# The attention's weighted sums in four visits per unit instead of eight, and one transpose a slot later

## The chip, the cores and the metric

The kernel runs on one core of one Trainium2 chip. The metric is device microseconds (us) of one execution. A profiled execution also has a span, from its first to its last instruction. The engines are TensorE (PE in the rows; PEld are its weight loads), VectorE (DVE), ScalarE (ACT), GpSimd (POOL) and SyncE (SP), which here issues every DMA.

## What is computed

Three layers in float32, one after the other: attention with rotary positions, an ELU feed-forward part, a bilinear feed-forward part.

```python
scores = scale * np.matmul(rotate(q), rotate(k).transpose(0, 1, 3, 2))   # [4, 8, 576, 576]
attn = np.exp(scores - np.max(scores, axis=-1, keepdims=True))
attn = attn / (np.sum(attn, axis=-1, keepdims=True) + 1e-09)
x = np.matmul(attn, v)                      # -> [2304, 512]
h = x @ w_in                                # [2304, 2048]
x = np.where(h > 0.0, h, np.exp(np.minimum(h, 0.0)) - 1.0) @ w_out
return ((x @ w1) * (x @ w2)) @ w3 @ w_out2  # [2304, 512]
```

## The kernel before

**Units and slots.** A unit of the attention is a batch and a pair of heads: 16 units. A unit has nine slots; a slot works on 128 queries of one head against all 576 keys, and the ninth on the last 64 queries of both heads. The code records the work slot by slot, and every engine executes its own instructions in the order in which they were recorded; in the attention no scheduler moves them. In slot n stand, in this order: the copies out of PSUM that slot n-1 left over (`evacuate_all`); the scores of slot n+2 (`scores`, tile `s`, TensorE L282, or L274 for the ninth slot); their maximum (`nm`, VectorE L294) and exponential with its sum (`pr`, ScalarE L298); the tasks that the tables below give to slot n; and at the end the transposes of the probabilities of slot n itself (`turn`, tile `ptp`, TensorE L330, and for the last 64 keys `ptl`, L338 and L342). Their copies to SBUF, `ptT` and `plT` (L312 on ScalarE, L314 on VectorE), follow at the head of the next slot.

```python
            for kc in range(4):
                at_ = kc * P + j * SK
                pe.transpose(pt[:, kc], pr[:, at_:at_ + P], idt)
```

The tiles `s` have two buffers in PSUM, so the scores of slot n+2 write the buffer that the exponential of slot n has read. The tiles `ptp`, `ptl`, `ptr` share two other buffers, so each waits until the copy out of an earlier one is done.

**The weighted sums.** For the first 256 queries of a unit (half 0) and the other 320 (half 1), `weigh` multiplies the turned probabilities with v: for key parts 0 to 3 two matmuls, one per head, each with 64 columns of weights (L388, 128\*64 in the rows); for key part 4 one matmul with 128 columns (L390) and in half 1 two of 64\*64 (L393). All add up in one PSUM tile `o`. In the slot after key part 4, VectorE multiplies `o` by the turned reciprocals `R` into `xT` (`weighed`, L402).

```python
            if kc < 4:
                for j in range(2):
                    pe.matmul(o[64 * j:64 * j + 64], vj[:, j, kc], th[:, j, kc], start=(kc == 0), stop=False)
                return
            pe.matmul(o[:, :256], vs[u][:, 2 * NKC * D:], tl[:, :256], start=False, stop=not hf)
            ...
            at(n + 1, weighed, u, hf)
```

**The reciprocals.** VectorE takes the reciprocals of the sums (`ri`, L353 and L354, in slots 2 and 7), GpSimd spreads them (`rb`, L81, slots 3 and 9), TensorE turns them (`ptr`, L371, slots `NTURN`), ScalarE copies them out (`R`, L375).

**The next unit's keys and queries.** GpSimd turns them by their positions (L180, L183) and splits them (L189); `stack` then sends them through eight DMAs from SBUF to SBUF (`st`, L256 and L259), the first four for the unit's first head, the others for its second. The scores of slots 7 and 8 are the first two of the next unit and need them.

A slot number above 8 in a table lies in the next unit: slot 10 of one unit is slot 1 of the next. In this document slots are counted from 0 to 8.

**After the attention** stands the first feed-forward part. Its instructions are ordered by a scheduler, which puts its first projections (`h`, L532) among the attention's last slots. Its weights come as 64-bit words and are converted on VectorE (L107, L110, L113), ScalarE and GpSimd.

Of the kernel before, what the change touches and what calls it, by code (L numbers as in the profile page):

```python
# [14 lines left out]
PSUM = bass.MemoryType.PSUM  # L15
# [1 line left out]
B, H, S, D = 4, 8, 576, 64  # L17
NT, DM, FF, F2 = B * S, H * D, 2048, 1024
P = 128
NKC = 5  # parts of the keys, 128 and at the end 64  # L20
SK = S + 64  # the keys with the last 64 of them in front once more
SCALE = 1.0 / 8.0
SIGN = -(2**31)
PAIRS = ((0, 0), (0, 1), (1, 0))  # the products of (hi, lo) with (hi, lo) that float32 keeps

# Slots of a unit (a pair of heads) in the attention, counted from its first: 4 parts of the queries for each head, and
# the last 64 queries of both. Work on the unit itself:
NORM = (2, 7)  # reciprocals of the sums, of the first 256 queries and of the others
SPREAD = (3, 9)  # their broadcast over d
NTURN = (5, 11)  # its transpose  # L30
PV = (
    (5, 0, (0,)), (6, 0, (1,)), (7, 0, (2, 3)), (8, 0, (4,)),
    (10, 1, (0,)), (11, 1, (1,)), (12, 1, (2, 3)), (13, 1, (4,)),
)  # slot, part of the queries, parts of the keys
LOAD_V = 6  # and on those that follow it: loads, and the steps of the rope of k and q
LOAD_QK = 4
ROPE = ((-1, 0, 1, 1, 4), (-5, -4, -3, -3, 2))
STACK = 4
# The first unit, of which nothing runs ahead
FIRST = ((0, 1, 4), (0, 0, 0, 1, 2), (0, 0, 3, 3, 4), 2)  # L40
KD = 420  # keys from here on are turned by the second engine
WARM = 27
FILL = (4, 2, 2)
EVAC_ACT = (1, 0, 0, 1, 0, 0, 0, 0, 1, 0, 1, 0)  # which copies from PSUM are ScalarE's, in turn

# Weights: how many parts of w_in and w_out are split during the attention, from which slot on, and the steps' slots
PF, PF_AT, PF_STEP, STEPS, DLEAD = 5, 10, 9, (0, 1, 2, 2, 3, 8), 6
NA = 2 * PF
# In the last tile of tokens of the first feed-forward part: when the weights of the second are loaded, per part of f
LOAD_O = (0, 1, 1, 2, 3, 3, 4, 5)  # L50
LOAD_3, PART_W, LOAD_AB, AB_STEP = 5, 8, 10, 2
DEEP = 3  # parts of w3 held at once


@with_exitstack
def kernel(
# [10 lines left out]
    wr_p = ctx.enter_context(tc.tile_pool(name="wr", bufs=3))  # L67

    def split(dst, src, hi_eng, lo_eng):
        """dst[:, 0] = src to 12 bits, dst[:, 1] = the exact rest."""  # L70
        hi, lo = dst[:, 0], dst[:, 1]
        copy_hi(hi, src, hi_eng)
        lo_eng.tensor_tensor(lo, src, hi.bitcast(F32), op=ALU.subtract)  # L73
# [15 lines left out]
        return raw  # L89

    def weight_steps(at_, raw, put):
        """Float64 words to two tiles' worth of float32: 12 bits of 24, and the rest.

        The high word read as float32 has a float64 exponent's upper 8 bits: times 2**-112 it is
        rebased by -896 (what is too small for float32 goes to 0), and 3 bits to the left it is
        float32's layout, without the sign."""
        words = raw.bitcast(I32).rearrange("p (n t) -> p n t", t=2)
        lo, hi = words[:, :, 0], words[:, :, 1]
        r = wr_p.tile([P, 512], F32, tag="wr", name="wr")
        i = r.bitcast(I32)  # L100
        made = []

        def rebase():
            act.activation(r, hi.bitcast(F32), ACTF.Abs, scale=2.0**-112)  # L104

        def shift():
            dve.tensor_scalar(i, i, 3, None, op0=ALU.logical_shift_left)  # L107

        def low():
            dve.scalar_tensor_tensor(i, lo, 29, i, op0=ALU.logical_shift_right, op1=ALU.bitwise_or)  # L110

        def sign():
            dve.scalar_tensor_tensor(i, hi, SIGN, i, op0=ALU.bitwise_and, op1=ALU.bitwise_or)  # L113

        def high():
            made.append(slot(at_, F32R, [P, 2, 512], "w"))
            act.activation(made[0][:, 0], r, ACTF.Copy)  # L117
            put(made[0])

        def rest():  # L120
            pool.tensor_tensor(made[0][:, 1], r, made[0][:, 0].bitcast(F32), op=ALU.subtract)  # L121

        return rebase, shift, low, sign, high, rest
# [8 lines left out]
        load_w(2 * f, w_in[f], win, f)  # L132
        load_w(2 * f + 1, w_out[f], wout, f)

    # ------------------------------------------------ attention, and w3 @ w_out
    with ExitStack() as c1:
        pool1 = lambda name, bufs: c1.enter_context(tc.tile_pool(name=name, bufs=bufs, reuse_waits="tile"))
        qk_p = pool1("qk", 3)
# [31 lines left out]
        TAB = (slice(SK - S, SK), slice(0, SK))  # L170

        def rope(u, w):
            """Steps of the turn of q or k by their positions, and of its split."""
            if u not in hls:
                hls[u] = hl_p.tile([P, 2, 2 * SK], F32R, tag="hl", name="hl")
            hl, r = hls[u], raws[u, w]
            hi, lo = hl[:, 0, COLS[w]], hl[:, 1, COLS[w]]

            def turn(z):
                pool.tensor_tensor(r[:, z], r[:, z], tab[:, w, z, TAB[w]], op=ALU.mult)  # L180

            def add():
                pool.tensor_tensor(r[:, 0], r[:, 0], r[:, 1], op=ALU.add)  # L183

            def high():
                copy_hi(hi, r[:, 0], act)

            def low():
                pool.tensor_tensor(lo, r[:, 0], hi.bitcast(F32), op=ALU.subtract)  # L189
                if w == 0:  # L190
                    diagonal(u)

            return [lambda: turn(0), lambda: turn(1), add, high, low]

        def first_load(u):
            """In the order of their use: the first half of the scores, the other, and the other queries."""
            for w in (0, 1):
                raws[u, w] = qk_p.tile([P, 2, (S, SK)[w]], F32, tag="raw_qk", name="raw_qk", padded_shape=[P, 2, SK])
            for dst, src, at_, to in (
                (tab[:, 1], tables, 0, 352), (raws[u, 1], k[u[0], u[1]], 0, 352), (raws[u, 0], q[u[0], u[1]], 0, 256),  # L200
                (tab[:, 1], tables, 352, SK), (raws[u, 1], k[u[0], u[1]], 352, SK), (raws[u, 0], q[u[0], u[1]], 256, S),
            ):
                nc.sync.dma_start(dst[:, :, at_:to], src[:, :, at_:to])

        def part(u, w, at_, to, eng, hi_eng, lo_eng):
            """Steps for some columns; the scale goes with the split."""
            s, c, t = (SCALE, 1.0)[w], COLS[w].start, TAB[w].start

            def turn(z):
# [30 lines left out]
                    pieces[k_]()  # L240

        def diagonal(u):
            """The last 64 queries of each head, against its own keys only."""
            for j in range(2):
                h = slice(64 * j, 64 * j + 64)
                copy_hi(diag[units.index(u) % 2][h, :, h], hls[u][h, :, 512:S].bitcast(F32), pool)

        def stack(u):
            """Of each head [128 = (q_hi, q_lo)], [k_hi, k_lo] and [k_lo, k_hi], on the partitions."""
            st = stacks[u] = st_p.tile([P, 2, 3, S], F32R, tag="st", name="st")  # L250
            for j in range(2):
                c = (SK, S)[j]
# [5 lines left out]
                    part = hls[u][64 * j:64 * j + 64, 1 - e].bitcast(F32)  # L258
                    nc.sync.dma_start(st[64 * e:64 * e + 64, j, 2].bitcast(F32), part[:, c:c + S])  # L259

        # ---- attention: of a pair of heads 128 queries each, and then the 64 last of both at once
        HALF = ((0, 256), (256, 320))
        sums_t, S_t, pr_t, pt_t = {}, {}, {}, {}

        def scores(g):
            u, c, j = g
            s = S_t[g] = ps_s.tile([P, 2, 512], F32, tag="s", name="s")
            if c == 4 or u == units[0]:
                # the halves one by one: of both heads with the diagonal, or of one
                d, h = diag[units.index(u) % 2], slice(64 * j, 64 * j + 64) if c < 4 else slice(0, P)  # L270
                at_ = S + 64 * (c == 4 or j == 0)
                for i, (a, e) in enumerate(PAIRS):
                    for n in range(2):
                        pe.matmul(  # L274
                            s[:, n, :288], hls[u][h, a, c * P:c * P + P] if c < 4 else d[:, a],
                            hls[u][h, e, at_ + n * 288:at_ + (n + 1) * 288], start=(i == 0), stop=(i == 2),
                        )
                return
# [123 lines left out]
            dve.tensor_tensor(xT[:, u[1], n0:n0 + nq], o_t.pop((u, hf)), R_t.pop((u, hf)), op=ALU.mult)  # L402

        def paced(n, i_, to, key, src):
            """The weights of src, fetched ahead of slot n, and the split's steps in the slots from there."""
            steps, raw = [], []

            def fetch():
# [56 lines left out]
        warm = cst.tile([P, P], F32, name="warm")  # L465

        def warm_up(n):
            """Keeps TensorE's clock up while it would wait."""
            ps = ps_t.tile([P, 512], F32, tag="pt", name="warm") if n else None
            for _ in range(n):  # L470
                pe.matmul(ps[:, :P], warm, warm, start=True, stop=True)
# [32 lines left out]
                    turn(seq[n])  # L504
                n += 1

    # ------------------------------------------------ the two feed-forward parts
    with ExitStack() as c2:
        pool2 = lambda name, bufs: c2.enter_context(tc.tile_pool(name=name, bufs=bufs, reuse_waits="tile"))
        xt_p = pool2("xt", 4)  # L510
# [14 lines left out]
            return ts  # L525

        def project(ps, w, x, n):
            """ps = (w as [c, 128 of f]).T @ x"""
            i = 0
            for cc in range(4):  # L530
                for a, c in PAIRS:
# [51 lines left out]
                load_w(8 + 2 * (i % DEEP) + z, w3[i][:, 512 * z:512 * z + 512], w3_t, (i, z))  # L583

        def part_w(i):
            """Rows of w3 @ w_o2."""
            ps = ps_h.tile([P, 512], F32, tag="h", name="w")
            for j in range(8):
                for n, (a, c) in enumerate(PAIRS):
# [140 lines left out]
```

## Time and profile before

| | |
|---|---|
| time, median of 3 runs (lowest, highest) | 1089.44 us (1088.63, 1090.51) |
| span of the profiled execution | 1087.1 us |
| median less span: what lies around the span | 2.3 us |
| granted TensorE clock, mean over the span | 0.986 of full speed |
| busy: PE, DVE, ACT, POOL | 1048.0, 621.9, 467.3, 365.4 us |
| attention | to about 317 us |
| first feed-forward part, weights still being converted | to about 400 us |

The profiled execution has no time of its own but its span, so the median less the span stands for what lies around it. A row of the trace's timeline reads: start, duration, engine, line, operation, what it writes and reads, shape, how many were merged; in brackets, where given, how long the engine was idle before and what ended that. Matmuls overlap, and their durations are modelled; TensorE's pace is read from the start of one group to the start of the next.

### The profile page before, as it was taken

Reading aid. Unit: us, or ns where it says so; the run is one execution under the profiler, and the core shown is the slowest. Engines: PE = TensorE matmul, PEld = TensorE weight load, DVE = VectorE, ACT = ScalarE, POOL = GpSimd, SP = SyncE. Lnnn points to the kernel's source line nnn. Section 1 sums busy time; section 2 is a strip of 40 time slices with the busy share of each in tenths; the row PEclk is TensorE's granted clock in tenths of the full one; section 3 lists DMA queues with packets and bytes.
Section 4 is the critical chain, followed back from the end, with each engine's and each line's share of the span. In section 5 each row is a group of like instructions: output and inputs, shape, how many; then the busy total and the mean of one; then the engine's idle time right before and its main releaser. Section 6 shows DMA issues by size and latency. Waiting matters only on the chain. (4 is left out here: it accounts for less than half of the span.)

```text
span 1087.1 us, 14661 instructions
## 1 busy us (share of the span) xinstructions
PE 1048.0 (96%) x5590; PEld 865.3 (80%) x5590; DVE 621.9 (57%) x982; ACT 467.3 (43%) x921; POOL 365.4 (34%) x336
## 2 busy tenths in 40 slices
PE   9999999999998789999999999889899999999998
PEld 7777677677766568888888999778788888889997
DVE  5778788777659975335335346997971313122211
ACT  3566667666636554334334335654451111112121
POOL 5788898877226551001000001343450000000000
PEclk7899999999999999999999999999999999999999
DMA  5777787867481000000000005446500100001000
GB/s 164 207 223 222 216 226 224 220 195 198 120 339 48 0 1 1 1 1 1 1 1 1 1 1 159 122 127 190 159 20 1 39 1 25 15 1 39 1 30 30
DMA packets 34870, 96.90 MB, mean 89 GB/s; under 512 B 4208, under 2 KB 5872, under 8 KB 34800
## 3 DMA queue, kind: packets, MB, share of 16 engines
q1 hardware_dynamic: 34800, 95.96, 29.6%
q8 instruction: 44, 0.72, 0.3%
q14 instruction: 26, 0.21, 0.1%
HBM read 64.68 MB, written 4.72 MB: 64 GB/s over the span
## 5 line engine op out<-in xcount | busy, mean ns | idle before, releaser
L559 PE MATMUL y<-g,w 128*128 128x512 f32 (+1 forms) x960 | 218.0, 374 | 23.8 <-ACT g L77 16.8
L559 PEld LDWEIGHTS y<-g,w 128*128 128x128 f32 x960 | 176.3, 191 | 54.8 <-ACT g L77 22.0
L532 PE MATMUL h<-xt,w 128*128 128x512 f32 (+1 forms) x960 | 212.2, 368 | 1.1 <-DVE e L547 1.1
L532 PEld LDWEIGHTS h<-xt,w 128*128 128x128 f32 x960 | 175.1, 188 | 24.8 <-DVE e L547 1.5
L73 POOL TENSOR_TENSOR xt<-xT,xt 128x512 fp32r<-128x512 f32 (+1 forms) x20 | 25.5, 1273 | 446.1 <-DVE xt L79 446.1
L298 ACT ACTIVATE pr<-s,nm 128x576 f32<-128x576 f32 x144 | 107.0, 743 | 101.8 <-DVE nm L294 100.9
L121 POOL TENSOR_TENSOR w<-wr,w 128x512 fp32r<-128x512 f32 x72 | 102.5, 1424 | 124.6 <-ACT w L117 119.8
L294 DVE TENSOR_REDUCE nm<-s 128x1 f32<-128x576 f32 x144 | 108.6, 754 | 24.8 <-PE s L282 12.0
L634 DVE TENSOR_TENSOR a<-b,a 128x512 f32<-128x512 f32 (+1 forms) x40 | 25.5, 637 | 157.5 <-PE b L532 156.8
L532 PE MATMUL a<-xt,w 128*128 128x512 f32 (+1 forms) x480 | 107.8, 368 | 2.7 <-DVE xt L73 2.7
L532 PE MATMUL b<-xt,w 128*128 128x512 f32 (+1 forms) x480 | 106.8, 367 | 0.0
L647 PE MATMUL y<-W,g 128*128 128x512 f32 x432 | 105.2, 391 | 0.2 <-DVE g L73 0.2
L544 ACT ACTIVATE e<-e 128x512 f32<-128x512 f32 (+1 forms) x80 | 47.0, 588 | 135.7 <-DVE e L543 135.6
L532 PEld LDWEIGHTS a<-xt,w 128*128 128x128 f32 x480 | 88.1, 188 | 15.5 <-DVE xt L73 3.1
L330 PEld LDWEIGHTS ptp<-idt,pr 128*128 128x128 f32 x576 | 63.4, 144 | 46.2 <-issue 24.7
L282 PE MATMUL s<-st 128*128 128x288 f32 x480 | 95.1, 316 | 4.0 <-DMA st<-hl 3.8
L532 PEld LDWEIGHTS b<-xt,w 128*128 128x128 f32 x480 | 87.6, 188 | 11.3
L330 PE MATMUL ptp<-idt,pr 128*128 128x128 f32 x576 | 96.4, 291 | 0.0
L647 PEld LDWEIGHTS y<-W,g 128*128 128x128 f32 x432 | 80.8, 188 | 16.7 <-DVE g L73 0.6
L543 DVE TENSOR_SCALAR e<-h 128x512 f32<-128x512 f32 (+1 forms) x80 | 50.6, 633 | 63.1 <-PE h L532 62.9
L547 DVE SCALAR_TENSOR_TENSOR e<-h,e 128x512 f32<-128x512 f32 (+1 forms) x80 | 50.7, 634 | 57.7 <-ACT e L545 57.7
L180 POOL TENSOR_TENSOR raw_qk<-raw_qk,tab 128x640 f32<-128x640 f32 (+1 forms) x56 | 82.5, 1482 | 2.3
(302 smaller groups left out, 1371.1 us busy)
## 6 DMA issues: line engine op xcount, KB each, us to landing
st<-hl SPq DMA_DIRECT2D x60, 288.0 KB, 4.5
raw<-w_ SPq DMA_DIRECT2D x32, 512.0 KB, 4.1
raw_qk<-k_ SPq DMA_DIRECT2D x15, 640.0 KB, 5.7
raw_qk<-q_ SPq DMA_DIRECT2D x15, 576.0 KB, 5.2
st<-hl SPq DMA_DIRECT2D x60, 144.0 KB, 4.2
raw<-w_in_ SPq DMA_DIRECT2D x16, 512.0 KB, 5.1
raw<-w_out_ SPq DMA_DIRECT2D x16, 512.0 KB, 5.8
out_<-ev SPq DMA_DIRECT2D x18, 256.0 KB, 2.1
```

What stands on the lines that cost most here:

```text
L121: pool.tensor_tensor(made[0][:, 1], r, made[0][:, 0].bitcast(F32), op=ALU.subtract)
L180: pool.tensor_tensor(r[:, z], r[:, z], tab[:, w, z, TAB[w]], op=ALU.mult)
L282: pe.matmul(s[:, n, :288], st[:, j, 0, c * P:c * P + P], st[:, j, z, n * 288:(n + 1) * 288], start=(z == 1), stop=(z == 2),)
L294: dve.tensor_reduce(nm, s[:, :, :288], axis=AX.XY, op=ALU.max, negate=True)
L298: act.activation(pr_t[u, c][:, j].rearrange("p (n i) -> p n i", n=2), s[:, :, :288], ACTF.Exp, bias=nm, accum_out=sums_t[u, hf][:, at_:at_ ...
L330: pe.transpose(pt[:, kc], pr[:, at_:at_ + P], idt)
L532: pe.matmul(ps[:, :n], w[:, a, cc * P:(cc + 1) * P], x[cc][:, c], start=(i == 0), stop=(i == 11))
L543: dve.tensor_scalar(e, ps[:, :n], 0.0, None, op0=ALU.min)
L544: act.activation(e, e, ACTF.Exp)
L547: dve.scalar_tensor_tensor(g, ps[:, :n], 0.0, e, op0=ALU.max, op1=ALU.add)
L559: pe.matmul(ys[ti][o][:, :n], wout[f][:, a, o * P:(o + 1) * P], g[:, c], start=(f == 0 and i == 0), stop=(f == NF - 1 and i == 2),)
L647: pe.matmul(outs[ti][o], g[:, a, o * P:(o + 1) * P], wW[f][:, c], start=(f == 0 and i == 0), stop=(f == NG - 1 and i == 2),)
```

## The change

Two tables of slots change. Half 0's key parts went to slots 5, 6, 7 and 8, and half 1's to slots 1, 2, 3 and 4 of the next unit; now they go to slots 5 and 7, and 1 and 3. Half 0's reciprocals are turned in slot 6, not 5. `weighed` follows `weigh` by a slot, so it moves from slot 0 to slot 8 for half 0, and from slot 5 to slot 4 for half 1.

```diff
-NTURN = (5, 11)  # its transpose
+NTURN = (6, 11)
 PV = (
-    (5, 0, (0,)), (6, 0, (1,)), (7, 0, (2, 3)), (8, 0, (4,)),
-    (10, 1, (0,)), (11, 1, (1,)), (12, 1, (2, 3)), (13, 1, (4,)),
-)  # slot, part of the queries, parts of the keys
+    (5, 0, (0, 1)), (7, 0, (2, 3, 4)), (10, 1, (0, 1)), (12, 1, (2, 3, 4)),
+)
```

The rest of the diff takes out comments; most lines stand one number lower after it.

TensorE around the border of two units, before (from slot 7's sums to slot 1's; `v__1550` are the unit's values):

```order
L388 MATMUL o<-ptT,v__1550 64x256 x4
L330 MATMUL ptp<-idt,pr 128x128 x4
L338 MATMUL ptl__1817<-idt,pr 128x128 x2
L282 MATMUL s<-st 128x288 x4
L390 MATMUL o<-plT,v__1550 128x256
L330 MATMUL ptp<-idt,pr 128x128 x4
L342 MATMUL ptl__1837<-idt,pr 64x128
L282 MATMUL s<-st 128x288 x4
L330 MATMUL ptp<-idt,pr 128x128 x4
L282 MATMUL s<-st 128x288 x4
L388 MATMUL o<-ptT,v__1550 64x320 x2
```

and after the change, the same place:

```order
L387 MATMUL o<-ptT,v__1547 64x256 x4
L389 MATMUL o<-plT,v__1547 128x256
L329 MATMUL ptp<-idt,pr 128x128 x4
L337 MATMUL ptl__1818<-idt,pr 128x128 x2
L281 MATMUL s<-st 128x288 x4
L329 MATMUL ptp<-idt,pr 128x128 x4
L341 MATMUL ptl__1838<-idt,pr 64x128
L281 MATMUL s<-st 128x288 x4
L329 MATMUL ptp<-idt,pr 128x128 x4
L281 MATMUL s<-st 128x288 x4
L387 MATMUL o<-ptT,v__1547 64x320 x4
```

The 128-column matmul of key part 4 has moved ahead of slot 7's transposes, slots 8 and 0 hold only scores and transposes, and slot 1 holds twice as many sums.

VectorE at the same place, before (the two `plT` copies belong to the transposes of slots 7 and 8):

```order
L314 COPY plT<-ptl__1817 128x256
L294 TENSOR_REDUCE nm<-s 128x1
L314 COPY plT<-ptl__1837 64x128
L294 TENSOR_REDUCE nm<-s 128x1
L402 TENSOR_TENSOR xT<-o,R 128x256
L294 TENSOR_REDUCE nm<-s 128x1
```

and after the change:

```order
L313 COPY plT<-ptl__1818 128x256
L293 TENSOR_REDUCE nm<-s 128x1
L401 TENSOR_TENSOR xT<-o,R 128x256
L313 COPY plT<-ptl__1838 64x128
L293 TENSOR_REDUCE nm<-s 128x1 x2
```

The multiplication into `xT` now stands ahead of the second `plT` copy.

TensorE in the last unit (`v__3599`), where the scheduler fills in the first projections `h`, before:

```order
L388 MATMUL o<-ptT,v__3599 64x256 x4
L330 MATMUL ptp<-idt,pr 128x128 x4
L532 MATMUL h<-xt,w 128x512 x16
L338 MATMUL ptl__3816<-idt,pr 128x128 x2
L390 MATMUL o<-plT,v__3599 128x256
L330 MATMUL ptp<-idt,pr 128x128 x4
L532 MATMUL h<-xt,w 128x512 x17
L342 MATMUL ptl__3827<-idt,pr 64x128
L532 MATMUL h<-xt,w 128x512 x4
L388 MATMUL o<-ptT,v__3599 64x320 x2
```

and after the change:

```order
L387 MATMUL o<-ptT,v__3596 64x256 x4
L389 MATMUL o<-plT,v__3596 128x256
L531 MATMUL h<-xt,w 128x512 x4
L329 MATMUL ptp<-idt,pr 128x128 x4
L531 MATMUL h<-xt,w 128x512 x12
L337 MATMUL ptl__3817<-idt,pr 128x128 x2
L531 MATMUL h<-xt,w 128x512 x8
L329 MATMUL ptp<-idt,pr 128x128 x4
L531 MATMUL h<-xt,w 128x512 x10
L341 MATMUL ptl__3828<-idt,pr 64x128
L531 MATMUL h<-xt,w 128x512 x11
L387 MATMUL o<-ptT,v__3596 64x320 x4
```

Ahead of the last half's sums stood 37 projections, and 45 stand there now.

## Rows read from the trace of the kernel before

**Rows 1.** The page: busy time of each engine (share of the span), instructions.

```profile
PE 1048.0 (96%) x5590; PEld 865.3 (80%) x5590; DVE 621.9 (57%) x982; ACT 467.3 (43%) x921; POOL 365.4 (34%) x336
```

**Rows 2.** Timeline of TensorE, 146.7 to 151 us: slots 8, 0 and 1.

```profile
146.76 0.77 PE L282 MATMUL s<-st 128*128 128x288 f32 x4
147.36 0.59 PE L390 MATMUL o<-plT,v__1550 128*128 128x256 f32 x2
147.79 0.60 PE L330 MATMUL ptp<-idt,pr 128*128 128x128 f32 x4
...
148.26 0.78 PE L282 MATMUL s<-st 128*128 128x288 f32 x4
148.88 0.66 PE L330 MATMUL ptp<-idt,pr 128*128 128x128 f32 x4
149.29 0.78 PE L282 MATMUL s<-st 128*128 128x288 f32 x4
150.00 0.76 PE L388 MATMUL o<-ptT,v__1550 128*64 128x320 f32 x4
150.69 0.66 PE L330 MATMUL ptp<-idt,pr 128*128 128x128 f32 x4
```

**Rows 3.** Timeline of TensorE, 153.9 to 156 us: slots 3 and 4.

```profile
153.98 1.30 PE L388 MATMUL o<-ptT,v__1550 128*64 128x320 f32 x8
155.21 0.66 PE L330 MATMUL ptp<-idt,pr 128*128 128x128 f32 x4
...
155.84 0.77 PE L282 MATMUL s<-st 128*128 128x288 f32 x4
```

**Rows 4.** Timeline of VectorE, 145.9 to 150 us: slots 7, 8 and 0.

```profile
145.97 0.74 DVE L353 TENSOR_SCALAR ri<-sums 128x5 f32<-128x5 f32 x1
...
147.04 0.42 DVE L314 COPY plT<-ptl__1817 128x256 f32<-128x256 f32 x1
147.56 0.76 DVE L294 TENSOR_REDUCE nm<-s 128x1 f32<-128x576 f32 x1
148.54 0.28 DVE L314 COPY plT<-ptl__1837 64x128 f32<-64x128 f32 x1 [0.22 <-PE ptl__1837 L342]
...
149.75 0.41 DVE L402 TENSOR_TENSOR xT<-o,R 128x256 f32<-128x256 f32 x1
```

**Rows 5.** Timeline of ScalarE, the end of slot 8's exponential, and slot 4.

```profile
149.00 0.19 ACT L298 ACTIVATION_READ_ACCUMULATOR pr<-s,nm 128x1 f32 x1
...
155.91 0.60 ACT L312 ACTIVATE ptT<-ptp 128x512 f32<-128x512 f32 x1
```

**Rows 6.** The tile `st`, 30 to 300 us: TensorE idle for it (us, times).

```profile
  DMA st<-hl: 7.0, 13
```

**Rows 7.** Timeline of TensorE: scores of slot 2 in two units, of slot 8.

```profile
133.97 0.78 PE L282 MATMUL s<-st 128*128 128x288 f32 x4
...
151.10 0.77 PE L282 MATMUL s<-st 128*128 128x288 f32 x4
...
164.56 0.51 PE L282 MATMUL s<-st 128*128 128x288 f32 x2 [0.19 <-DMA st<-hl]
```

**Rows 8.** Timeline of GpSimd, 135 to 152.6 us.

```profile
135.99 0.49 POOL L81 TENSOR_SCALAR rb<-ri 128x256 f32<-128x256 f32 x1 [1.61 <-DVE ri L354]
...
145.41 1.28 POOL L121 TENSOR_TENSOR w<-wr,w 128x512 fp32r<-128x512 f32 x1
147.09 0.93 POOL L81 TENSOR_SCALAR rb<-ri 128x256 f32<-128x256 f32 x3 [0.41 <-PE ptl__1817 L338]
...
150.98 1.56 POOL L189 TENSOR_TENSOR hl<-raw_qk,hl 128x640 fp32r<-128x640 f32 x1
```

**Rows 9.** Timeline of SyncE, 152 to 161.5 us: the queries' load, the last stack DMAs.

```profile
152.57 0.60 SPq L163 DMA_DIRECT2D raw_qk<-q_  x1
...
159.63 2.56 SPq L259 DMA_DIRECT2D st<-hl  x2
```

**Rows 10.** Timeline of TensorE in the last unit, 300 to 318 us.

```profile
303.62 3.90 PE L532 MATMUL h<-xt,w 128*128 128x512 f32 x16
```

**Rows 11.** Timeline of VectorE in the last unit, 300 to 318 us.

```profile
317.56 0.49 DVE L402 TENSOR_TENSOR xT<-o,R 128x320 f32<-128x320 f32 x1 [4.28 <-PE o L393]
317.97 0.68 DVE L543 TENSOR_SCALAR e<-h 128x512 f32<-128x512 f32 x1
```

**Rows 12.** Windows: busy us (instructions) of PE, PEld, DVE, ACT, POOL; clock; DMA.

```profile
340.00:400.00 60.00, 44.78 (x182) 32.73 (x182) 57.10 (x67) 34.83 (x59) 37.80 (x27) 1.00 0.00 0
```

## The prediction

> **What bounds the kernel now.** I began with the page: TensorE is busy 96% of the span and no other engine more than 57% [rows 1]. So a us of TensorE work saved in the attention should be a us of the span, unless TensorE then waits. The change takes no matmul away; it only moves groups between slots. So I next read the timeline of TensorE, engine against engine, over one unit without a stall (134 to 151 us), taking its pace from the starts of its groups. The thing to see is slots 8, 0 and 1 [rows 2]: the second plT copy ends at 148.54 + 0.28 = 148.82 [rows 4], and the transposes that reuse its PSUM buffer start at 148.88, 0.06 later. The exponential of slot 8's scores ends at 149.00 + 0.19 = 149.19 [rows 5], and the scores that overwrite them start at 149.29, 0.10 later. TensorE shows no idle time there, but its partners finish just as it arrives. Third, I read who waits for the stack DMAs: TensorE sat idle 7.0 us in 13 places for them [rows 6], in about every second unit. Last came the first feed-forward part: from 340 to 400 us VectorE is busy 57.1 of 60 us and TensorE 44.8 [rows 12], so that stage follows VectorE.
>
> **Term 1, fewer visits.** A visit of four 64-column matmuls takes 0.69 (150.00 to 150.69) [rows 2], and one of eight 1.23 (153.98 to 155.21) [rows 3]. Four more cost 0.54, so 0.15 of a visit does not depend on how many there are. Going in costs too: from scores to sums 0.71 (149.29 to 150.00), from scores to transposes 0.62 (148.26 to 148.88) [rows 2], 0.09 more. Each half unit loses one visit (three become two; I take the 256-query half at the same price): 2 x 0.24 = 0.48 us a unit, and once less at the end, where the last half's visits already stand together: 15.5 x 0.48 = **-7.4 us**. Bounds: 0.15 to 0.24 a visit, -4.7 to -7.4.
>
> The Trainium skill, TensorEngine Tiling (Array Packing), Key Properties, says that a change of tiling mode drains the engine; the 0.24 us agrees, and by that rule alone the change would be worth the whole of term 1. The same page, PSUM Bottleneck, warns that a faster TensorE does not speed up the copies out of PSUM, which speaks against the change; term 2 is such a case in rows.
>
> **Term 2, the two bare slots.** The 128-column matmul (147.36 to 147.79, 0.43) [rows 2] leaves slot 8, so slots 8 and 0 hold only scores and transposes. From slot 8's scores to slot 1's scores TensorE now takes 149.29 - 146.76 = 2.53; without the 0.43 it would be there after 2.10. I work out when it may go, in us after slot 8's scores start:
> - The first transposes wait for the first plT copy, which ends at 147.46 [rows 4], 0.70; with 0.06 they start at 0.76 (0.62 without the wait).
> - Their last 64 keys are ready for VectorE 148.54 - 147.79 = 0.75 later, 1.51. VectorE's maximum runs from 0.80 to 1.56 [rows 4].
> - Now the multiplication into xT stands ahead of the copy. It takes 0.41 [rows 4]; VectorE starts an instruction about 0.08 before the one ahead of it ends (317.56 + 0.49 against 317.97 [rows 11]). So it ends at 1.89, and the copy runs from 1.81 to 2.09.
> - Slot 0's transposes start at 2.15, slot 1's scores 0.41 later (148.88 to 149.29), at 2.56.
>
> 2.56 against 2.10: 0.46 us of waiting a unit, 15 borders of units: **+6.9 us**. Even without xT in the way the exponential holds slot 1's scores until 149.19 - 146.76 = 2.43, so the wait is at least 0.33, +5.0. Above, the wait could be 0.65, +9.8, by the last rival.
>
> **Term 3, slot 4.** It loses both its sums, and its transposes come right behind its scores: 0.62 after 155.84, 156.46 [rows 3]. They reuse the buffer that ScalarE's ptT copy frees at 155.91 + 0.60 = 156.51 [rows 5], plus 0.06: 0.11 late, 15 times: **+1.6 us** (0 to 1.6).
>
> **Term 4, the stack DMAs.** GpSimd starts a unit's round with the reciprocals of slot 2: scores at 133.97 [rows 7], rb at 135.99 after 1.61 of waiting. From there to the end of the keys' split it is nearly without pause, 150.98 + 1.56 = 152.54 [rows 8]. At 152.57 SyncE may issue the queries' load, then eight stack DMAs [rows 9]; TensorE goes on with the second half of slot 8's scores at 164.56, the landing [rows 7]. That is 30.59 us from slot 2 to slot 8 of the next unit. Without a stall TensorE takes 17.13 for the unit (133.97 to 151.10 [rows 7]) and 13.13 more to that second half (146.76 - 133.97, and 0.34 for half of the scores): 30.26, so it waits some 0.3; the unit after a wait has that much slack, hence every second one. After the change the unit takes 17.13 - 0.48 + 0.46 + 0.11 = 17.22. The way from slot 2 to slot 8 shrinks more, because 0.54 of sums moved into slot 1, ahead of slot 2: 13.13 - 0.48 - 0.54 + 0.43 + 0.11 = 12.65. Together 29.87, so the wait is 0.72, 0.4 more per pair of units; or nothing more, if GpSimd loses its 0.41 wait ahead of the second rb [rows 8], since those reciprocals come some 0.9 earlier against its round. I take the middle, 0.2, for six pairs: **+1.1 us** (0 to 2.3).
>
> **Term 5, the end of the attention.** VectorE works in order; its multiplication of the last half waited 4.28 us for TensorE's last sums, and all the feed-forward work behind it begins at 317.97 [rows 11]. Now 45 projections stand ahead of these sums, not 37. Eight at 3.90 / 16 = 0.24 [rows 10] are **+1.9 us** of delay, and since VectorE is what that stage follows, it lasts to the end (0 if the stage hides it; the scheduler also shuffles the weights' conversion, which I bound at 2 us either way).
>
> **Free.** The turn of the reciprocals and its copy go one slot later; what needs them is the multiplication two slots on. The second multiplication moves from slot 5 to 4, behind a maximum. SyncE's and GpSimd's order in the attention does not change.
>
> **Sum.** -7.4 + 6.9 + 1.6 + 1.1 + 1.9 = **+4.1**: span 1087.1 + 4.1 = 1091.2, with the 2.3 between span and median 1093.5 us. The bounds, all one way, give -7.4 + 5.0 = -2.4 at the low side and -4.7 + 9.8 + 1.6 + 2.3 + 1.9 at the high side, +10.9.
>
> **Rivals.**
> - *It pays (faster).* The buffers come free in time, say because TensorE reaches slot 8 later than I think and finds the copies done. Then terms 2 to 4 vanish: -7.4 + 1.9 = -5.5, 1084.0 us. For it: no idle time in rows 2. Against it: 0.06 and 0.10 us of slack, where 0.43 is taken away. It is decided at the transposes of slot 0: they must start within 1.7 to 1.8 us of slot 8's scores. The Trainium skill's rule on tiling modes (TensorEngine Tiling, Key Properties), taken alone, gives this rival.
> - *No change.* Terms 2 and 3 eat term 1, and terms 4 and 5 are hidden: 0 to +1.1, about 1090 us. For it: both are read from work that only one rare place shows.
> - *VectorE held up in slot 7 (slower still).* The reciprocals' first instruction took 0.74 and ended with GpSimd's conversion, 145.41 + 1.28 = 146.69 [rows 4, 8]. It now comes about 1 us earlier in GpSimd's round and can be held by two GpSimd instructions; then the first plT copy starts 0.2 to 0.4 late and the chain of term 2 with it. At 0.19 a unit this is +2.9, 1096.4 us. Against it: reciprocals that come early may slip in between two of GpSimd's.
>
> **How the numbers follow.** Forecast 0.48, held-up VectorE 0.12, no change 0.27, it pays 0.13. What a measurement of this kernel can tell from no change is about 0.2%, 2.2 us. So slower 0.60, same 0.27, faster 0.13. The range leaves out the faster case and the far end of the slow one: 1088.5 to 1097.5 us.
>
> **What would show it.** Right: slots 8 and 0 with TensorE idle for VectorE's plT copy, some 0.4 us a unit; about 2.55 us from slot 8's scores to slot 1's; a unit still 17.1 to 17.3 us long; idle time for the stack DMAs above 7.0 us; the last xT about 3.5 us later than 317.56. Wrong: 2.1 to 2.2 us from slot 8 to slot 1 (term 2 does not exist), or an xT that ends later but a feed-forward part that ends as before (term 5 hidden).

## The result and the profile after

The changed kernel took 1097.72 us (median of 6 runs, 1092.12 to 1099.73) against 1089.04 for the kernel before (6 runs, 1086.09 to 1092.52): a ratio of 1.0076, 95% interval [1.0052, 1.0099]. It is slower, as forecast, but by 0.76% where the forecast was 0.38%, and 0.2 us above the upper end of the range. The profiled execution has a span of 1095.7 us (1087.1 before). Line numbers of the attention and behind are lower by 1 than before.

TensorE is still busy 96% of the span; the page alone does not tell the two kernels apart:

```profile
PE 1051.8 (96%) x5590; PEld 873.1 (80%) x5590; DVE 620.9 (57%) x982; ACT 467.3 (43%) x921; POOL 363.7 (33%) x336
```

To find where 8.6 us went, take the same instruction in every unit as a mark, the small transpose of the second reciprocals in slot 2 of the next unit (`ptr<-two`). First and last mark in the kernel before, timeline of TensorE (the last one taken is the 15th of 16, since behind it projections stand among the attention's slots):

```profile
45.48 0.33 PE L373 MATMUL ptr<-two,rb 128*128 128x64 f32 x2
...
292.41 0.33 PE L373 MATMUL ptr<-two,rb 128*128 128x64 f32 x2
```

And TensorE in the changed kernel: the marks (two of them, 245.00 and 262.30, bound a unit without a stall, 17.30), slot 4 (249.05), slots 7 to 1 of one unit without a stall (254.44 to 259.13, to be held against [rows 2]), and what follows the last sums:

```profile
48.41 0.33 PE L372 MATMUL ptr<-two,rb 128*128 128x64 f32 x2
...
245.00 0.33 PE L372 MATMUL ptr<-two,rb 128*128 128x64 f32 x2
...
249.05 0.76 PE L281 MATMUL s<-st 128*128 128x288 f32 x4
249.76 0.66 PE L329 MATMUL ptp<-idt,pr 128*128 128x128 f32 x4
...
254.44 1.08 PE L387 MATMUL o<-ptT,v__2934 128*64 128x256 f32 x8
255.46 0.70 PE L389 MATMUL o<-plT,v__2934 128*128 128x256 f32 x2
255.99 0.60 PE L329 MATMUL ptp<-idt,pr 128*128 128x128 f32 x4
256.43 0.38 PE L337 MATMUL ptl__3195<-idt,pr 128*128 128x128 f32 x2
256.56 0.78 PE L281 MATMUL s<-st 128*128 128x288 f32 x4
257.33 0.66 PE L329 MATMUL ptp<-idt,pr 128*128 128x128 f32 x4
...
257.85 0.77 PE L281 MATMUL s<-st 128*128 128x288 f32 x4
258.72 0.66 PE L329 MATMUL ptp<-idt,pr 128*128 128x128 f32 x4
259.13 0.76 PE L281 MATMUL s<-st 128*128 128x288 f32 x4
...
262.30 0.33 PE L372 MATMUL ptr<-two,rb 128*128 128x64 f32 x2
...
296.92 0.33 PE L372 MATMUL ptr<-two,rb 128*128 128x64 f32 x2
...
326.87 5.49 PE L531 MATMUL h<-xt,w 128*128 128x512 f32 x12 [2.93 <-DVE e L546]
```

VectorE in the changed kernel: the copies of slots 8 and 0 with the multiplication between them, then the last multiplication into xT, and the sixth minimum of the feed-forward part:

```profile
256.85 0.42 DVE L313 COPY plT<-ptl__3195 128x256 f32<-128x256 f32 x1 [1.15 <-PE ptl__3195 L337]
...
258.06 0.41 DVE L401 TENSOR_TENSOR xT<-o,R 128x256 f32<-128x256 f32 x1
258.39 0.27 DVE L313 COPY plT<-ptl__3215 64x128 f32<-64x128 f32 x1
...
323.17 0.49 DVE L401 TENSOR_TENSOR xT<-o,R 128x320 f32<-128x320 f32 x1 [6.22 <-PE o L392]
...
348.52 0.68 DVE L542 TENSOR_SCALAR e<-h 128x512 f32<-128x512 f32 x1
```

The end of the first tile of tokens is ScalarE's first copy out of `y`. Before, and in the changed kernel:

```profile
419.40 1.07 ACT L565 ACTIVATE xT<-y 128x512 f32<-128x512 f32 x2
```

```profile
428.76 0.60 ACT L564 ACTIVATE xT<-y 128x512 f32<-128x512 f32 x1 [4.86 <-PE y L558]
```

Idle time for the stack DMAs, the view of the tile `st` [rows 6]:

```profile
  DMA st<-hl: 8.7, 11
```

The account of the two profiled executions, in us:

| stretch | before | after | difference |
|---|---|---|---|
| start to the first mark | 45.48 | 48.41 | +2.9 |
| first to last mark, 14 units | 246.93 | 248.51 | +1.6 |
| last mark to the start of the last xT | 25.15 | 26.25 | +1.1 |
| end of the last xT to the first copy of y | 101.35 | 105.10 | +3.75 |
| from there to the end | 667.7 | 666.9 | -0.8 |

The first line can't be put down to the change. Two kernels below (12 and 4 idle matmuls at the attention's end) have the changed kernel's program up to there, and their first marks stand at 47.89 and 42.11, with a granted clock of 0.54 and 0.83 from 10 to 40 us. Without that line these two executions differ by 5.7 us. The fourth line is the largest, and the prediction had no term for it. It had, in brackets, 2 us either way for a reordered conversion of weights.

### The profile page after: what moved, and what is told of

Its sections match the earlier page's. It is cut to its first block, busy times and chain, and to the rows that moved or that the text cites. A ratio compares the mean times of both kernels' runs of the same rounds, so it can differ in the third digit from the quotient of the medians.

```text
span 1095.7 us, 14677 instructions
## 1 busy us (share of the span) xinstructions
PE 1051.8 (96%) x5590; PEld 873.1 (80%) x5590; DVE 620.9 (57%) x982; ACT 467.3 (43%) x921; POOL 363.7 (33%) x336
## 5 line engine op out<-in xcount | busy, mean ns | idle before, releaser
L531 PE MATMUL h<-xt,w 128*128 128x512 f32 (+1 forms) x960 | 216.1, 373 | 2.9 <-DVE e L546 2.9
L531 PEld LDWEIGHTS h<-xt,w 128*128 128x128 f32 x960 | 177.7, 191 | 27.6 <-DVE e L546 3.4
```

The source lines that it names most:

```text
L531: pe.matmul(ps[:, :n], w[:, a, cc * P:(cc + 1) * P], x[cc][:, c], start=(i == 0), stop=(i == 11))
```

## The experiments

All ratios are to the kernel before on the same chip. "To y" is the time from the end of the last xT to the first copy of y in the profiled execution; "clean unit" is the period of a late unit, between two marks, without a stall; "14 units" is the time from the first mark to the last, stalls and units with weights included, in one profiled execution each.

| kernel | median | ratio, 95% interval | clean unit | 14 units | to y |
|---|---|---|---|---|---|
| before | 1089.04 | 1 | 17.10 | 246.9 | 101.35 |
| changed | 1097.72 | 1.0076 [1.0052, 1.0099] | 17.31 | 248.5 | 105.10 |
| turn alone | 1089.88 | 1.0004 [0.9986, 1.0023] | 17.10 | 244.5 | 101.37 |
| sums alone | 1091.53 | 1.0017 [0.9999, 1.0034] | 17.51 | 248.5 | 101.30 |
| xT a slot later | 1093.73 | 1.0037 [1.0017, 1.0057] | 17.26 | 245.7 | 104.21 |
| 12 idle matmuls | 1092.43 | 1.0032 [1.0015, 1.0049] | 17.31 | 248.7 | 101.39 |
| 4 idle matmuls | 1098.10 | 1.0074 [1.0051, 1.0098] | 17.31 | 248.3 | 106.34 |
| parts 4 apart | 1090.86 | 1.0006 [0.9987, 1.0025] | 17.2, with a stall | 245.8 | 101.32 |
| parts 4 apart, late spreading | 1100.11 | 1.0096 [1.0070, 1.0123] | 16.6 | 259.0 | 101.35 |
| before, late spreading | 1088.43 | 0.9981 [0.9960, 1.0003] | 17.10 | 247.9 | 101.39 |
| late spreading in units 11 to 15 | 1089.86 | 1.0013 [0.9992, 1.0035] | 16.6 | 244.6 | 101.35 |
| late spreading, steps a slot earlier | 1090.44 | 1.0002 [0.9983, 1.0022] | 16.6 | 249.4 | 101.34 |

**The turn alone.**

```diff
-NTURN = (5, 11)
+NTURN = (6, 11)
```

> The kernel before with the one change that the first half's reciprocals are turned a slot later, the sums in eight visits as before. Theory (the prediction held this part to be free): the kernel before, 1089 us, within 1 us, with 17.1 us a unit. Rival (the turn's two transposes fill a slot that was full, or its copy comes late for the multiplication): 17.2 to 17.3 us a unit, 2 to 3 us slower than the kernel before, and part of what I put down to the visits is this.

No difference: alone the turn is free, as the prediction held. Beside the merged visits it isn't, as the next run shows.

**The sums alone**, with the turn back in slot 5.

```diff
-NTURN = (6, 11)
+NTURN = (5, 11)
```

> The other half of the change: the sums in four visits as in the changed kernel, the first half's reciprocals turned in slot 5 as before. In it the scheduler puts the instructions of VectorE behind the last sums in the same order as in the kernel before; in the changed kernel that order is another one, in which the fifth conversion of a weight comes ahead of the activation. Theory (that order costs 3.7 us up to the first tile of tokens): a unit without a stall 17.3 us as in the changed kernel, from the last xT to the first copy of y 101.4 us as before and not 105.1, the whole 1093 to 1094 us. Rival (it is the 2.9 us in which TensorE idles behind the last sums, and the clock that falls there): 104 to 105 us, the whole 1097 us.

To y it is 101.30 us, as the theory of the order wants, and the whole came out 2 us better than expected. The unit was a miss: 17.51, not 17.3. TensorE in slots 5 and 6:

```profile
250.20 0.38 PE L370 MATMUL ptr<-idt,rb 128*128 128x128 f32 x2
250.51 1.08 PE L387 MATMUL o<-ptT,v__2939 128*64 128x256 f32 x8
...
251.94 1.03 PE L273 MATMUL s<-hl,diag 128*128 128x288 f32 x6
252.96 0.33 PE L329 MATMUL ptp<-idt,pr 128*128 128x128 f32 x1
```

The turn stands ahead of a 64-column visit and takes 0.31 to its start, where ahead of transposes it takes 0.22; and six scores take 1.02 to the transposes behind them, where they took 0.88 to the turn. So the later turn, worth nothing alone, is worth 0.2 us a clean unit beside the merged visits. Over 14 units both take 248.5 us all the same: the matmuls of the slower unit wait less for stack DMAs (1.9 us, and 3.9 in the changed kernel). What the turn does cost is the order behind the attention: with it the kernel is 1.0076 of the one before, without it 1.0017.

**The multiplication into xT a slot later** (first half), so that the second plT copy is not behind it.

```diff
-            at(n + 1, weighed, u, hf)
+            at(n + 2 - hf, weighed, u, hf)
```

> The changed kernel, but the first half's multiplication into xT goes one slot later, behind slot 0's maximum, so that the second plT copy no longer stands behind it on VectorE. Theory (term 2): the copy ends some 0.4 us earlier, slot 0's transposes follow at once, and only the exponential holds slot 1's scores: 2.43 us from slot 8's scores to slot 1's in place of 2.57, 17.18 us a unit in place of 17.31, 2 us less than the changed kernel in all. Rival (the transposes of slot 0 wait for something else than this copy, or the multiplication now holds slot 0's work just as long): 2.55 to 2.6 us and no difference to the changed kernel.

TensorE, slots 8, 0 and 1:

```profile
234.99 0.78 PE L281 MATMUL s<-st 128*128 128x288 f32 x4
...
236.27 0.78 PE L281 MATMUL s<-st 128*128 128x288 f32 x4
236.89 0.66 PE L329 MATMUL ptp<-idt,pr 128*128 128x128 f32 x4
237.49 0.80 PE L281 MATMUL s<-st 128*128 128x288 f32 x4
```

And ScalarE, the end of slot 8's exponential:

```profile
237.24 0.19 ACT L297 ACTIVATION_READ_ACCUMULATOR pr<-s,nm 128x1 f32 x1
```

Slot 0's transposes now follow their scores after 0.62 (0.87 in the changed kernel), so xT was the cause of that wait. Slot 1's scores start at 237.49, 0.06 after the exponential's end at 237.24 + 0.19. From slot 8's scores it is 2.50, where 2.43 was expected and 2.57 stood before. The second buffer takes about half of the gain back, and a unit gains 0.05, not 0.13: the chain was right, its second member is worth more than I gave it. The median is 4 us below the changed kernel's, where 2 were expected; 14 clean units at 0.05 are 0.7 of it, to y it is 0.9 less, and the rest, mostly fewer stalls in the profiled execution, is not traced to this edit.

**Twelve idle matmuls behind the last sums, and four.** They compute nothing that is read.

```diff
+            warm_up(12)
```

> The changed kernel, and behind the last sums of the attention TensorE gets 12 matmuls of 128 columns on a constant tile, whose product nobody reads (about 2 us, by 0.66 us for four such transposes), in place of 2.9 us of idle time ahead of the 4th projection behind the sums. Theory (the idle time at 324 us brings the granted clock down to 0.5, seen there from 325.8 to 332.6 and again at 356.6 and 377.0, and TensorE then falls behind VectorE): no stretch at 0.5 between 320 and 400 us, and the time from the last xT to the end 3 us shorter, 1094 to 1095 us where the changed kernel has 1097.7. Rival (that stage follows VectorE, and the clock there costs nothing; or the clock falls anyway): the time of the changed kernel, within 1 us.

> The changed kernel with 4 idle matmuls of 128 columns behind the last sums in place of 12. The order on VectorE stays that of the changed kernel (with 12 it became that of the kernel before, so that run could not tell the two apart), and TensorE's idle time falls to about 2.4 us, what it is in the kernels in which only the turn is moved or the parts 4 stand apart (2.47, where the first copy of y came 101.3 us after the last xT). Theory (the order): 104 to 105 us from the last xT to the first copy of y, the whole 1096 to 1098 us. Rival (the idle time and the clock): 101.4 us, the whole 1093 to 1094 us.

The run with 12 looked like a proof of the clock: 5 us less, and no stretch at half clock until 353.5 us. But it had changed two things, as the order of VectorE's instructions shows. Its sixth minimum starts 22.22 us after the last xT, and 25.35 (348.52 - 323.17) in the changed kernel:

```profile
322.81 0.49 DVE L401 TENSOR_TENSOR xT<-o,R 128x320 f32<-128x320 f32 x1 [6.22 <-PE o L392]
...
345.03 0.68 DVE L543 TENSOR_SCALAR e<-h 128x512 f32<-128x512 f32 x1
```

Nine kernels, the one before among them, have one order on VectorE behind the last xT, and take 101.30 to 101.39 to y. The changed kernel and the one with 4 idle matmuls have another, the one with xT later a third; these take 104.21 to 106.34. ScalarE's and GpSimd's orders up to y change in the same three kernels and agree in the nine, so what differs is the scheduler's order on all three. The run with 4 separates that order from the clock. TensorE's idle time there was shorter, the granted clock stayed at 1.00 for 25 us, and y came later still. TensorE, ScalarE, and the windows (columns as in [rows 12]):

```profile
320.31 3.04 PE L532 MATMUL h<-xt,w 128*128 128x512 f32 x12 [2.04 <-DVE e L547]
```

```profile
423.43 0.60 ACT L565 ACTIVATE xT<-y 128x512 f32<-128x512 f32 x1 [4.86 <-PE y L559]
```

```profile
317.10:342.10 25.00, 21.47 (x93) 16.33 (x91) 23.62 (x30) 15.22 (x27) 14.03 (x9) 1.00 0.46 170
```

The same stretch in the changed kernel, where the clock did fall:

```profile
323.66:348.66 25.00, 22.07 (x86) 17.75 (x85) 23.62 (x30) 15.26 (x27) 14.02 (x9) 0.86 0.44 169
```

VectorE is busy 23.62 of 25 us in both: it is the bound, so half clock on TensorE costs nothing there, and what counts is which of its instructions come first. The turn alone is the other half of the proof: it has the order of before and three stretches at half clock, and takes 101.37. My theory of the clock fell. (With 4, a stretch at half clock does come later, at 397.9 us; whether the 1.2 us above the changed kernel are its work, no run shows.)

The traces also show where the order's 3.75 us are lost. VectorE's waits from the last xT to the first copy of y, before and in the changed kernel (us in total, times, longest):

```profile
DVE e L543 <- PE h L532: 5.5, 2, 3.6
```

```profile
DVE e L542 <- PE h L531: 10.8, 3, 5.0
```

All of these waits stand behind the last conversion of this stretch, where none is left to fill VectorE's time, and with the new order it waits for TensorE's projections 5.3 us longer. The sums alone, with the order of before, wait 5.5 again.

**The parts 4 apart**: merged 64-column visits, the 128-column matmuls back behind the scores of slots 8 and 4.

```diff
-    (5, 0, (0, 1)), (7, 0, (2, 3, 4)), (10, 1, (0, 1)), (12, 1, (2, 3, 4)),
+    (5, 0, (0, 1)), (7, 0, (2, 3)), (8, 0, (4,)), (10, 1, (0, 1)), (12, 1, (2, 3)), (13, 1, (4,)),
```

> The changed kernel, but the part 4 of each half (128 columns) goes back to slots 8 and 4, where it stood before; the merged 64-column visits stay. Theory (terms 1 to 3): slots 8 and 0 are covered again, so slot 8's scores to slot 1's take 2.53 us or a little less, slot 4 loses its 0.1 of waiting, and the fewer visits are left alone: a unit without a stall takes 17.13 - 0.48 = 16.65 us, 0.66 less than the 17.31 of the changed kernel, and the whole about 1085 us where the kernel before has 1089. Rival (a visit costs only its fixed 0.15, entering and leaving are not saved by merging, and the stack DMAs take what is gained): a unit of 16.8 to 17.0 us, the idle time for the stack DMAs above 9 us, the whole 1088 to 1091.

The whole came out as the rival has it, 1091 us, with 12.1 us of idle time for the stack DMAs by the view of [rows 6]; a unit, 17.2, is longer than either expected. Half of the rival's reason holds, the stack DMAs took the gain; the other half, a smaller price of a visit, does not, as the late spreading below shows. In every late unit TensorE now waits for a stack DMA in slot 8; TensorE there:

```profile
269.32 0.51 PE L281 MATMUL s<-st 128*128 128x288 f32 x2
270.23 0.51 PE L281 MATMUL s<-st 128*128 128x288 f32 x2 [0.40 <-DMA st<-hl]
```

Followed back: SyncE issues all of those DMAs but the first from 261.50, when GpSimd has split the queries (260.06 + 1.41); GpSimd had idled ahead of that split, since the spreading of the reciprocals stood in front of it, and those come at TensorE's pace:

```profile
259.69 0.40 POOL L80 TENSOR_SCALAR rb<-ri 128x256 f32<-128x256 f32 x1 [2.44 <-DVE ri L353]
260.06 1.41 POOL L188 TENSOR_TENSOR hl<-raw_qk,hl 128x576 fp32r<-128x576 f32 x1
```

The reciprocals are ready at 259.53 (259.35 + 0.18), the DMA's data at 270.23: 10.70 us. TensorE needs 6.54 from there to the next reciprocals, and the sum, 17.24, is the unit. (The sum must be the unit; that each step on the way waits for the one ahead is what makes it a loop.)

**Late spreading**, to break that loop; and the same alone in the kernel before.

```diff
-SPREAD = (3, 9)
+SPREAD = (4, 9)
```

> The kernel with merged visits and the parts 4 in slots 8 and 4, and GpSimd's spreading of the first half's reciprocals moved from slot 3 to slot 4, behind the split of the queries. In that kernel TensorE waited in every late unit 0.3 to 0.4 us for a stack DMA; GpSimd idled 2.44 us ahead of that split, for the reciprocals of slot 2 that the spreading ahead of it needs. Theory (the wait is a loop: reciprocals, spreading, split, stack DMAs 10.70 us, then TensorE 6.54 us to the next reciprocals, 17.24 in all, whatever the sums cost): late units without the wait, 16.6 to 16.7 us, and the whole 1086 us or less, faster than the kernel before. Rival (SyncE's queue of eight stack DMAs and the loads, or the rest of GpSimd's round, holds the unit at 17.2 anyway): 17.1 to 17.25 us and 1089 to 1091 us as without this move.

> The control to it: the kernel before with nothing but the spreading of the first half's reciprocals in slot 4. Theory: late units stay at 17.1 us, since TensorE does not wait for the stack there; in the units with weights the idle time for the stack DMAs, 7.0 us, falls by 0 to 2 us: 1087 to 1089.5 us, within the noise of the kernel before. Rival (the spreading's place is worth as much here, and the gain of the merged kernel is not from the visits): 1085 us or less.

In late units the theory holds in part: the four behind the weights took 17.17, 16.63, 18.13 and 16.60 us, the two long ones with TensorE waiting for stack DMAs again (0.3 and 0.7 us), so the wait is rarer, not gone. TensorE, slots 8, 0 and 1, without a wait:

```profile
298.95 0.77 PE L281 MATMUL s<-st 128*128 128x288 f32 x4
299.56 0.59 PE L389 MATMUL o<-plT,v__3380 128*128 128x256 f32 x2
...
301.49 0.78 PE L281 MATMUL s<-st 128*128 128x288 f32 x4
```

The kernel as a whole lost, though: nine of the ten units ahead of these took 19.2. VectorE's conversion steps, in ns (shortest/median/longest), from 60 to 235 us; the middle step with the early spreading, then all three with the late one:

```profile
L109 DVE SCALAR_TENSOR_TENSOR wr<-raw,wr x9: 1002/1006/1331, 67.2 to 208.9; 128x512 int32<-128x512 int32 x9
```

```profile
L106 DVE TENSOR_SCALAR wr<-wr x9: 395/1431/1434, 65.9 to 217.9; 128x512 int32<-128x512 int32 x9
L109 DVE SCALAR_TENSOR_TENSOR wr<-raw,wr x9: 682/1869/1872, 68.5 to 220.5; 128x512 int32<-128x512 int32 x9
L112 DVE SCALAR_TENSOR_TENSOR wr<-raw,wr x9: 693/1923/1931, 70.4 to 222.4; 128x512 int32<-128x512 int32 x9
```

Without GpSimd's pause the steps meet its two-operand instructions. VectorE and GpSimd in such a unit:

```profile
162.80 1.86 DVE L109 SCALAR_TENSOR_TENSOR wr<-raw,wr 128x512 int32<-128x512 int32 x1
164.70 1.93 DVE L112 SCALAR_TENSOR_TENSOR wr<-raw,wr 128x512 int32<-128x512 int32 x1
166.55 0.41 DVE L313 COPY plT<-ptl__1933 128x256 f32<-128x256 f32 x1
```

```profile
162.57 3.51 POOL L179 TENSOR_TENSOR raw_qk<-raw_qk,tab 128x640 f32<-128x640 f32 x2
```

The copy behind them comes late, and TensorE's transposes wait 0.53 for it at 167.02, and its next scores 0.87 for the exponential at 168.55. The control moved by -0.19%, its interval just reaching no change; the place of the spreading alone is not what makes the late units 16.6.

**Two mended versions**: late spreading only in the units without weights, and late spreading everywhere with the conversion a slot earlier.

```diff
-                at(n + SPREAD[hf], spread, u, hf)
+                at(n + SPREAD[hf] + (hf == 0 and i > 10), spread, u, hf)
```

```diff
-PF, PF_AT, PF_STEP, STEPS, DLEAD = 5, 10, 9, (0, 1, 2, 2, 3, 8), 6
+PF, PF_AT, PF_STEP, STEPS, DLEAD = 5, 9, 9, (0, 1, 2, 2, 3, 8), 6
```

> The kernel with merged visits and the parts 4 in slots 8 and 4, and the first half's reciprocals spread a slot later in units 11 to 15 alone, in which no weights are converted. Theory (late units: the loop through GpSimd is broken; units with weights keep the earlier order, in which VectorE's three conversion steps take 0.40, 1.01 and 0.69 us and not 1.43, 1.87 and 1.92): units with weights as in the kernel with the parts 4 apart (17.15 to 17.9), the three periods behind them 16.6 us each in place of 17.2, 2 us less than that kernel, about 1088.5 us, 0.1% below the kernel before. Rival (the late units' gain comes back as a stack wait in the next one, as 18.13 us once did): 17.2 us on average and 1090.5 us.

> The kernel with merged visits, the parts 4 apart and the late spreading in all units, and the steps of the weights' conversion one slot earlier, so that VectorE meets GpSimd's pause ahead of the queries' split (1.24 us in slot 2) and not its two multiplications of 128x640 behind the spreading. Theory (the 19.24 us of a unit with weights are VectorE's conversion steps held up by GpSimd): at least two of the three steps take 0.4 to 0.7 us again, and these units 16.7 to 17.3 us; the whole 1080 to 1086 us. Rival (they meet another of GpSimd's instructions, whatever their slot, since GpSimd is busy 16 of 17 us): steps of 1.4 to 1.9 us and units above 18 us; the whole 1095 us or more.

In the first the late units came to 16.59, 16.64, 16.99 and 16.59 us, as expected, but the units with weights still waited for the stack, and the median is no better than before. In the second two of the three steps are short again (medians 1.46, 0.77 and 0.69 us), but they stand ahead of a ptT copy, for which TensorE's weight loads wait 0.9 to 1.1 us: units of 17.7, and two of 19.6 and 20.3, not the 16.7 to 17.3 expected. Neither version beats the kernel before.

## Why the prediction was right, and where its sizes were off

The direction and the mechanism of terms 1 to 3 held; the sum left out one effect that it had named, the order behind the attention.

**Term 1** (-0.48 a unit) holds where the 128-column matmul stands behind scores and no stack DMA is waited for: 17.10 becomes 16.6. In the changed kernel it stands directly behind a 64-column visit and takes longer there, which my price left out: from its start to the transposes 0.53 (255.46 to 255.99) where 0.43 stood in [rows 2], and as much in the other half. So -0.27 a unit was saved.

**Term 2**: forecast 2.56 us from slot 8's scores to slot 1's, measured 2.57 (256.56 to 259.13), in the order forecast: maximum, xT, copy, transposes. Without the waits it is 2.11, from late spreading: 301.49 - 298.95, less the 0.43. The wait is thus 0.46, as forecast.

**Term 3**: slot 4's transposes come 0.71 after their scores (249.05 to 249.76), 0.09 late; forecast 0.11.

With 0.06 given back in slot 7, where transposes behind the 128-column matmul take 0.44 to the next group and not 0.50, a unit is -0.48 + 0.21 + 0.46 + 0.09 - 0.06 = +0.22, measured +0.21; forecast +0.09.

**Term 4** did not come, and its sign is open. 14 units at +0.21 would be +2.9; they took +1.6, so what they lose beyond clean units fell from 7.5 to 6.2 us. By the view of [rows 6] the idle time rose from 7.0 to 8.7, the sign that was named; but that view counts one wait twice, at the matmul and at its weight load. Of the matmuls alone, 9 waited 3.8 us before and 6 waited 3.9 after. One profile of a kernel doesn't decide it either: the turn alone, with the same 17.10, loses 5.1 us, not 7.5. The loop, found only when TensorE was made faster, says how near the limit was. Its 17.24 us belong to the kernel with the parts 4 apart, in which slot 1's eight sums lie in it, and is no floor for the kernel before, whose units take 17.10; but in that kernel's late units the last stack DMA landed only 0.2 to 0.8 us ahead of the scores that need it, and in the changed one's 0.2 to 0.3. A prediction that prices a saving should look for such a loop as the floor of the gain.

**Term 5**: +1.1 from the last mark to the last xT, +1.9 forecast. That the delay lasts to the end held: to y it is 101.3 us in nine kernels, whose last xT starts anywhere from 317 to 330 us.

**The step that failed in size** is the bracket in term 5, "the scheduler also shuffles the weights' conversion, which I bound at 2 us either way". It measured 3.75 us in the profiles. In the medians, the changed kernel and the one with 12 idle matmuls (same units, the order of before) differ by 0.44%, 4.8 us. With the order of before the change costs 0.32%, 3.5 us, close to the sum of +4.1. That is partly luck: the unit cost 0.12 more than forecast, 1.7 us over 14, and the +1.1 of term 4 did not come. About half of the whole is thus the order (3.75 of 8.6 us in the profiles, 4.8 of 8.7 in the medians, whose ratios are known to about 0.2%), which I had left out of the sum and of the range. The line "Free" failed with it: beside these sums, the later turn tips that order.

**The rivals.** "It pays" fell at the place that was named: slot 0's transposes start 258.72 - 256.56 = 2.16 us after slot 8's scores, not at 1.7 to 1.8. Its saving existed (16.6), and no kernel here collected it in whole: the stack loop or VectorE held it. VectorE held up by GpSimd in slot 7 did not come: in the unit shown, which has no weights, the first copy starts at 256.85, waiting for TensorE alone, and in the units with weights VectorE also sat idle 0.2 to 1.0 us for TensorE ahead of it. The same collision, at another place, is what made late spreading slow. The 3.75 us of the other order end in VectorE's waits for projections, behind the conversions; which instruction's place decides stays open.

## What to carry to other kernels

Price a merged visit at both of its ends, and ask of every group that loses its neighbour which buffer it now reaches too early. Before a saving per round is multiplied by the rounds, look for loops through other engines that close within a round: their length, in the changed order, is the floor. And where a scheduler fills one stage with the next one's work, compare the order behind the edit too; an edit that moves no instruction there can still cost more than all that it moves.

## What the runs showed of the hardware

VectorE's integer steps, 0.40 and 0.69 us beside GpSimd's one-operand instructions, took 1.43, 1.87 and 1.92 in eight of nine units in which its two-operand instructions ran beside them. A stretch at half clock is not always lost time: from the last xT to y, a kernel that had three such stretches (turn alone, granted clock 0.5 for 3.4 us each) took 101.37 us, and the kernel before, with none, 101.35; VectorE was busy 23.6 to 24.8 us of every 25 there. And from 10 to 40 us the granted clock differs between runs of one program (0.54 and 0.83 above), and with it the first mark moves by 6 us.
